# A third set of seven-product tiles, scaling on GpSimd and regrouped loads in a retention and feed-forward kernel

## The chip, the cores and the metric

The kernel runs on one NeuronCore of one Trainium2 chip. The metric is the device time of one execution, in microseconds (us), as the median of several executions; the profile is that of one more execution, read by the hardware profiler. PE is the matrix engine, ACT the scalar engine, DVE the vector engine, POOL is GpSimd, SP the sync engine, which only issues DMAs here.

## The reference

A retention layer (attention without softmax, with a decay per head) feeds a feed-forward layer:

```python
scores = scale * np.matmul(q, k.transpose(0, 1, 3, 2))      # q, k, v: 8 x 8 heads x 576 x 64
Dmat = np.where(rel >= 0, gamma[:, None, None] ** rel, 0.0) # rel = query position - key position
attn = np.matmul(scores * Dmat, v)
x = attn.transpose(0, 2, 1, 3).reshape(4608, 512)
h = x @ w_in                                                # 512 x 2048
out = (h * sigmoid(1.702 * h)) @ w_out                      # 2048 x 512
```

## The kernel before

**Tiling.** The 4608 tokens are 36 units of 128 tokens (`NU`), four units make one of nine chunks (`NCH`, c0 to c8). Units 8, 17, 26 and 35 hold the last 64 tokens of two batch entries each; their loads are split in two DMAs and they leave no state behind. For a unit u the kernel loads k, q (cast to bf16) and v by DMAs from POOL's queue (`load`, L925; `load_kq` L228, `load_v` L244), transposes k and q together by one DMA from SP's queue (`dma_transpose`, L399, key `T{u % 8}`), and scales v by a decay factor into `vp` (`scale_v`, L353, one 128x512 operation on DVE). Retention is done for two units at a time (`block`, L898): products with the state kept so far (`inter`), products with the masked scores of these units (`values`), and, in the same stretch of PE, the scores and the state contributions of the two units after them (`ahead`, L882). So the attention stretch of units 2j and 2j+1 reads the transposes and scaled v of units 2j+2 and 2j+3. On DVE it leaves two operations `x_out_pair` (L550, into xT), four `state_sum` (L442, running sums in the ring `stm` of 8 slots) and two `scores_out` (L514, masked scores); the sums are cast on ACT into `kv` (`state_cast`, L454).

**Up stage.** The hidden values of a chunk are 16 F tiles (f0 to f15) of 128 features by 512 tokens. A plain tile (`up`, L562) takes four products of 128x512 and one gelu on ACT out of PSUM into gT. In chunks 2 to 8 f0 to f7 are done in two `UpSet`s (L776) of four tiles each, by a scheme with seven block products in place of eight, where each block product (`step` n, n = 0 to 6) is four matmuls of 128x256. The operands are sums and differences of blocks of x (`xsums`, L764, four DVE operations per chunk) and of w_in (`winsums`, L745, four DVE operations once). A set uses two PSUM banks: X and Y for the first, C and D for the second. ACT copies steps 0, 2 and 3 out to `part`; DVE adds steps 1, 4 and 5 to these parts (`comb`, L811); ACT then makes the gelus: `gelu_first`, that of step 6 straight from PSUM, and `gelu_last` over two parts at once (128x1024).

**Down stage.** The product with w_out takes seven block products as well (`Pair.run`, L703), d1 to d7 below, of 16 matmuls of 128x256 each, that alternate between the banks A and B (`turn`, L862). d1 and d2 read gT as it is; d3 to d7 read sums that DVE made of gT (`Pair.sums`, L656: four operations 0 to 3, done for groups of F tiles). d3 needs operation 1, d4 operation 0, d5 operation 2 (which overwrites part of gT), d6 operation 3. The results are copied by ACT or added by DVE into `osb`, of which SP stores the rows. Between the products a function `hook(i)` (L1171) places other work; one attention stretch stands after d3 (hook 2). In the last chunk the tokens are two `Pair`s of single units.

**Order.** The order of each engine's queue is the order in which these calls are written; `Program.op` (L41) adds only the semaphore waits. So a wait at the head of a queue holds everything behind it. In a chunk of `steady` (L1070) from c2 on, SP is given four transposes (units 4c+6 to 4c+9), POOL is given the loads of units 4c+10 to 4c+13 to start once the last of these transposes has landed, and the four `scale_v` stand among the `comb`s and behind them (L1132 to L1142). The up stage runs the steps of its sets in turn, then the plain tiles in the banks A and B, with an attention stretch after the second of them (f13 in c2, f9 later; L1143 to L1153). All four sum operations of each group are given to DVE at the end of the up stage.

Of the kernel before, what the change touches and what calls it, by code (L numbers as in the profile page):

```python
# [13 lines left out]
P = 128  # L14
# [146 lines left out]
def bass_retnet_parallel__then__act_gelu_quick_kernel(  # L161
# [8 lines left out]
    NLD, NVN, NVP, NQT, NKV = 12, 10, 8, 8, 16  # L170
    es = ExitStack()
    with es:
        def sb(name, shape, dtype):
            return es.enter_context(nc.sbuf_tensor(name, shape, dtype))
# [13 lines left out]
        stm = sb("stm", [P, 8, HP, DH], FP32)  # L188
# [5 lines left out]
        winsum = sb("winsum", [P, 4, 2, 4, P], BF16)  # L194
# [247 lines left out]
        def state_sum(u, a):  # L442
            if u >= NU or unit_info(u)[1] == 2:
                return
            i = 2 * u + a
            src = ps32(KB[a])[:, 256 * (u % 2) : 256 * (u % 2) + 256].rearrange("p (a i) -> p a i", i=DH)
            dst, prev = stm[:, i % 8, :, :], stm[:, (i - 1) % 8, :, :]
            if unit_info(u)[2] == 0 and a == 0:
                op("dve", lambda e: e.tensor_copy(dst, src), reads=[KB[a]], writes=[f"stm{i % 8}"])
            else:  # L450
                op("dve", lambda e: e.tensor_tensor(dst, src, prev, ALU.add),  # L451
                   reads=[KB[a], f"stm{(i - 1) % 8}"], writes=[f"stm{i % 8}"])
# [6 lines left out]
        def cast_range(i0, n):  # L459
            op("act", lambda e: e.activation(  # L460
                kv[:, i0 % NKV : i0 % NKV + n, :, :], stm[:, i0 % 8 : i0 % 8 + n, :, :], AF.Copy),
               reads=[f"stm{(i0 + i) % 8}" for i in range(n)],
               writes=[f"kv{(i0 + i) % NKV}" for i in range(n)])
# [175 lines left out]
        class Pair:  # L639
# [16 lines left out]
            def sums(self, f0, f1):  # L656
                k0, k1 = f0 // 2, f1 // 2
                a, g = (lambda r, c: self.gpart(r, c, f0, f1)), (lambda r, c: self.gkeys(r, c, f0, f1))
                s = lambda n: gsum[:, n, k0:k1, self.at : self.at + self.n]
                ks = lambda n: [f"gs{n}_{k}_{j}" for j in self.places() for k in range(k0, k1)]  # L660
                for d, kd, x, kx, y, ky, alu in (
                    (s(0), ks(0), a(1, 0), g(1, 0), a(1, 1), g(1, 1), ALU.add),
                    (s(1), ks(1), s(0), ks(0), a(0, 0), g(0, 0), ALU.subtract),
                    (a(1, 0), g(1, 0), a(0, 0), g(0, 0), a(1, 0), g(1, 0), ALU.subtract),
                    (s(2), ks(2), a(0, 1), g(0, 1), s(1), ks(1), ALU.subtract),
                ):
                    op("dve", lambda e, d=d, x=x, y=y, alu=alu: e.tensor_tensor(d, x, y, alu),  # L667
                       reads=kx + ky, writes=kd)
# [76 lines left out]
        def winsums():  # L745
            def w(r, h):
                return w_in_sb[:, slice(h, 4, 2), 0 : 8 * P].rearrange(
                    "p a (k r n) -> p a k r n", r=2, n=P)[:, :, :, r, :]

            def ws(n):  # L750
                return winsum[:, n, :, :, :]

            for n, x, y, alu in ((0, w(1, 0), w(1, 1), ALU.add), (1, ws(0), w(0, 0), ALU.subtract),
                                 (2, w(0, 0), w(1, 0), ALU.subtract), (3, w(0, 1), ws(1), ALU.subtract)):
                op("dve", lambda e, n=n, x=x, y=y, alu=alu: e.tensor_tensor(ws(n), x, y, alu),
                   reads=[f"win{f}" for f in range(8)] + {1: ["wi0"], 3: ["wi1"]}.get(n, []), writes=[f"wi{n}"])
# [19 lines left out]
        class UpSet:  # L776
# [26 lines left out]
            def part(self, n):  # L803
                return (part[:, n, 512 * self.s : 512 * self.s + 512],
                        [f"gs{n}_{k}_{j}" for k in range(4 * self.s, 4 * self.s + 4) for j in range(2)])
# [48 lines left out]
            def gelu_last(self):  # L854
                v = part[:, 1:3, 512 * self.s : 512 * self.s + 512].rearrange("p n (i t) -> p n i t", t=256)
                self.gelu(v, self.part(1)[1] + self.part(2)[1], None, 1)

        SETS = (("X", "Y"), ("C", "D"))
        last_store = {}
# [210 lines left out]
        def steady():  # L1070
            four = Pair(0, 2, 2)
            for c in range(1, NCH):
                if c == 1:
                    for u in range(10, 14):
                        load(u)
                    for u in range(8, 14):
                        dma_transpose(u, [f"vn{13 % NVN}"])
                    for u in (14, 15):
                        load(u, after=[f"T{9 % NQT}_0"])
                else:  # L1080
                    for u in range(16 if c == 2 else 4 * c + 6, min(4 * c + 10, NU)):
                        dma_transpose(u)
                    for u in range(4 * c + 10, 4 * c + 14):
                        load(u, after=[f"T{(4 * c + 9) % NQT}_0"])
                last = c == NCH - 1
                if c == 1:
# [21 lines left out]
                    for u in (14, 15):  # L1108
                        dma_transpose(u)
                    for u in (16, 17):  # L1110
                        load(u, after=[f"T{15 % NQT}_0"])
                else:
                    pairs = (Pair(3, 0, 1), Pair(1, 2, 1, 1)) if last else (four,)
                    vps = [u for u in range(4 * c + 6, 4 * c + 10) if u < NU]
                    sets = [UpSet(c, i, *banks) for i, banks in enumerate(SETS)]
                    f0 = 4 * len(sets)

                    def sums(f0, f1, which=pairs):
                        for pair in which:
                            pair.sums(f0, f1)  # L1120

                    if c == 2:
                        for lo in (0, 2):
                            for f in (f0, f0 + 2):
                                up_group(c, f, 2, lo, lo + 2, turn())
                    for n in range(7):
                        for w in sets:
                            w.step(n)
                        if c == 2 and n == 1:
                            now(rest)  # L1130
                            rest.clear()
                        if n in ((3, 4) if c == 2 else (1, 4)):  # L1132
                            for u in vps[:1]:
                                scale_v(u)
                            del vps[:1]
                        if c == 2 and n == 4:
                            state_cast(12, 14)
                        if n in (4, 5):
                            for w in sets[:-1] if n == 4 else sets[-1:]:
                                w.gelu_first()  # L1140
                    for u in vps:
                        scale_v(u)  # L1142
                    for f in range(12 if c == 2 else 8, NF):  # L1143
                        up(c, f, b=turn())
                        if f == (12 if c == 2 else 9):
                            sets[0].gelu_last()
                            if not last:
                                rest = block(2 * c + 2)
                                now(rest[:2])
                                del rest[:2]  # L1150
                                sets[1].gelu_last()
                                now(rest[:4])
                                del rest[:4]  # L1153
                        if last and f == 11:
                            sets[1].gelu_last()
                        if f == (13 if c == 2 or last else 11):
                            sums(0, 8)
                            if last or c == 2:
                                sums(8, 12)
                    if last:  # L1160
                        sums(12, 16, pairs[:1])
                    else:
                        sums(12 if c == 2 else 8, 16)
# [7 lines left out]
                def hook(i):  # L1171
                    if c == 1:
# [15 lines left out]
                        if i == 5:  # L1188
                            scale_v(12)
                            scale_v(13)  # L1190
# [5 lines left out]
                    if i == 0:  # L1196
                        cast_now()
                        now(rest)
                        rest.clear()
                    if i == 2 and 2 * (2 * c + 3) < NU:  # L1200
                        rest.extend(block(2 * c + 3))
                        now(rest[:2])
                        del rest[:2]
# [3 lines left out]
                    if i == 4:  # L1207
                        now(xsums(c + 1))
                        cast_now()
                    if i == 5:  # L1210
                        now(rest)
                        rest.clear()

# [64 lines left out]
```

## Time and profile before

| quantity | value |
|---|---|
| runs | 285.85, 286.57, 289.94 us; median 286.57 |
| the profiled execution, its own time | 289.0 us |
| its span, first to last instruction | 287.2 us |
| PE busy | 273.8 us, 95% of the span |
| DVE busy | 201.5 us, 70% |
| ACT busy | 150.2 us, 52% |
| POOL busy (issuing DMAs, nearly all) | 110.2 us, 38% |
| mean granted clock of PE | 0.994 |

Busy shares are means over stages that differ. In the timeline a row gives the start, the duration, the engine, the line, the operation and its tiles, and in brackets the idle time before it and who ended it. Matmuls are pipelined: a group of matmuls lasts, for what comes behind it, from its start to the start of the next group, which is less than the duration in its row. The same holds for ACT and DVE, where the next operation starts before the row's end.

### The profile page before, as it was taken

The page shows a single profiled execution, that of the slowest core. Times are in us where ns is not written, and L with a number is a line of the kernel's source. Part 1 is how long each engine was busy: PE and PEld are TensorE (multiplying, and loading weights), DVE is VectorE, ACT ScalarE, POOL GpSimd, SP SyncE. Part 2 cuts the span into 40 slices and gives each one's busy share as a digit, 9 for nine tenths or more (in the row PEclk, how much of TensorE's full clock was granted, in tenths as well). Part 3 has the DMA queues.
Part 4 walks back from the last instruction along what each step waited for, and adds up shares of the span by engine and source line. Part 5 has one row for each costly group of instructions (what it writes and reads, how often), then busy time and mean ns, then how long its engine had stood idle before and what let it go on. Part 6 is the DMA issues. An engine that isn't in the chain of part 4 may idle for free.

```text
span 287.2 us, 9444 instructions
## 1 busy us (share of the span) xinstructions
PE 273.8 (95%) x4202; PEld 202.7 (71%) x4202; DVE 201.5 (70%) x402; ACT 150.2 (52%) x266; POOL 110.2 (38%) x141
## 2 busy tenths in 40 slices
PE   8899999999879969999999999999999999999996
PEld 6575445788768548866885788479848884887475
DVE  5851657598658795789778977877787876745541
ACT  7456333663318822585368536842774288327821
POOL 9999878103308193008604920093053000000000
PEclk9999999999999997999999999999999999999999
DMA  9999999999999899499967996599788090012013
GB/s 167 183 201 206 201 234 243 242 139 149 141 229 192 99 159 135 147 151 97 198 213 107 152 121 169 129 141 157 236 95 113 2 205 19 2 41 108 0 25 124
DMA packets 116937, 40.73 MB, mean 142 GB/s; under 512 B 104096, under 2 KB 110240, under 8 KB 116896
## 3 DMA queue, kind: packets, MB, share of 16 engines
q0 software_dynamic: 79712, 22.82, 70.7%
q1 hardware_dynamic: 36896, 17.05, 26.3%
q8 instruction: 33, 0.54, 0.8%
q10 hardware_dynamic: 288, 0.26, 0.3%
q14 instruction: 8, 0.07, 0.1%
HBM read 36.70 MB, written 9.44 MB: 161 GB/s over the span
## 4 chain that ended last, share of the span: by engine, by line
PE 56%; POOL 20%; DMA 13%; DVE 5%; ACT 3%; issue 2%; SPq 0%; POOLq 0%; DVEq 0%
PE psA L685 14%; PE psB L685 14%; POOL kqn L236 10%; DMA vn<-in_v_dram 7%; PE psB L566 6%; PE psA L566 6%; POOL vn L249 5%; PE psC L799 4%; PE psX L799 4%; DMA kqn<-in_q_dram 3%; PE psD L799 3%; DVE part L667 3%; PE psY L799 3%; DMA kqT<-kqn 3%; POOL w_in_sb L271 3%; ACT gT L822 2%
## 5 line engine op out<-in xcount | busy, mean ns | idle before, releaser
L236 POOL DMA_DIRECT2D kqn<-in_k_dram x39 | 34.3, 884 | 107.0 <-DMA kqT<-kqn 104.0
L249 POOL DMA_DIRECT2D vn<-in_v_dram x40 | 36.5, 921 | 0.2
L236 POOL DMA_DIRECT2D kqn<-in_q_dram x37 | 32.7, 893 | 0.1
L566 PE MATMUL psB<-xT,w_in_sb 128*128 128x512 bf16 x120 | 30.9, 380 | 0.4 <-ACT gT L571 0.4
L566 PE MATMUL psA<-xT,w_in_sb 128*128 128x512 bf16 x120 | 30.9, 380 | 0.3
L698 ACT ACTIVATE osb<-psA 128x512 f32<-128x512 f32 (+1 forms) x19 | 10.5, 552 | 37.4 <-PE psA L685 37.3
L355 DVE TENSOR_TENSOR vp<-vn,vfac 128x512 bf16<-128x512 f32 x36 | 23.9, 684 | 6.1 <-DMA vn<-in_v_dram 6.1
L698 ACT ACTIVATE osb<-psB 128x512 f32<-128x512 f32 (+1 forms) x17 | 9.3, 547 | 36.0 <-PE psB L685 36.0
L554 DVE TENSOR_TENSOR xT<-psX,gq 128x512 bf16<-128x512 f32 x16 | 11.1, 691 | 22.9 <-PE psX L529 22.9
L822 ACT ACTIVATE gT<-part 128x512 bf16<-128x512 f32 (+1 forms) x28 | 22.2, 847 | 0.0
L460 ACT ACTIVATE kv<-stm 128x1024 bf16<-128x1024 f32 (+1 forms) x17 | 15.4, 903 | 11.9 <-DVE stm L451 11.9
L571 ACT ACTIVATE gT<-psA 128x512 bf16<-128x512 f32 x30 | 17.9, 596 | 6.8 <-PE psA L566 6.6
L571 ACT ACTIVATE gT<-psB 128x512 bf16<-128x512 f32 x30 | 17.9, 596 | 6.5 <-PE psB L566 6.5
L566 PEld LDWEIGHTS psB<-xT,w_in_sb 128*128 128x128 bf16 x120 | 10.4, 98 | 15.2 <-ACT gT L571 5.5
L566 PEld LDWEIGHTS psA<-xT,w_in_sb 128*128 128x128 bf16 x120 | 10.4, 98 | 14.5 <-ACT gT L571 5.0
L685 PE MATMUL psB<-wsum,part 128*128 128x256 bf16 x128 | 16.6, 280 | 3.0 <-DVE part L667 3.0
L685 PE MATMUL psA<-wsum,gT 128*128 128x256 bf16 x144 | 17.5, 273 | 1.0 <-issue 1.0
L685 PEld LDWEIGHTS psB<-wsum,part 128*128 128x128 bf16 x128 | 12.1, 99 | 5.7 <-DVE part L667 4.1
L685 PE MATMUL psA<-wsum,part 128*128 128x256 bf16 x128 | 15.7, 275 | 0.3 <-DVE osb L701 0.3
L685 PEld LDWEIGHTS psA<-wsum,gT 128*128 128x128 bf16 x144 | 14.0, 98 | 2.9 <-issue 1.2
L667 DVE TENSOR_TENSOR part<-gT 128x1024 bf16<-128x1024 bf16 (+2 forms) x21 | 11.7, 559 | 5.7 <-ACT gT L571 4.6
L685 PE MATMUL psB<-w_out_sb,gT 128*128 128x256 bf16 x128 | 15.4, 273 | 0.0
(151 smaller groups left out, 679.4 us busy)
## 6 DMA issues: line engine op xcount, KB each, us to landing
vn<-in_v_dram POOLq DMA_DIRECT2D x32, 256.0 KB, 5.0
out_dram<-osb SPq DMA_DIRECT2D x30, 256.0 KB, 2.5
kqn<-in_k_dram POOLq DMA_DIRECT2D x31, 128.0 KB, 4.6
kqn<-in_q_dram POOLq DMA_DIRECT2D x31, 128.0 KB, 4.9
w_out_sb<-in_moe_w_out_dram POOLq DMA_DIRECT2D x4, 512.0 KB, 14.1
out_dram<-osb SPq DMA_DIRECT2D x10, 128.0 KB, 2.4
w_in_sb<-in_moe_w_in_dram POOLq DMA_DIRECT2D x8, 128.0 KB, 5.3
w_in_sb<-in_moe_w_in_dram POOLq DMA_DIRECT2D x4, 256.0 KB, 7.9
```

The lines of the kernel that those rows point to most:

```text
L236: e.dma_start(kqn[sl][p0 : p0 + n, which, :, :], src[b, :, s0 : s0 + n, :].rearrange("h p d -> p h d"),)
L249: e.dma_start(vn[sl][p0 : p0 + n, :, :], v[b, :, s0 : s0 + n, :].rearrange("h p d -> p h d"))
L355: op(eng, lambda e: e.tensor_tensor(vp[u % NVP].ap(), vn[sl].ap(), vfac[:, ty, :, None].to_broadcast([P, H, DH]), ALU.mult), reads=[f"vn{s ...
L460: op("act", lambda e: e.activation(kv[:, i0 % NKV : i0 % NKV + n, :, :], stm[:, i0 % 8 : i0 % 8 + n, :, :], AF.Copy), reads=[f"stm{(i0 + i ...
L554: op("dve", lambda e: e.tensor_tensor(xT[ch % 2][:, slice(hh, 4, 2), P * jj : P * jj + 2 * P].rearrange("p g (u t) -> p u g t", u=2), ps32 ...
L566: op("pe", lambda e, a=a: e.matmul(bank[b][:, n0:n1], w_in_sb[:, a, P * f : P * f + P], xT[c % 2][:, a, n0:n1], start=(a == 0), stop=(a == ...
L571: op("act", lambda e: e.activation(gT[:, f, n0:n1], bank[b][:, n0:n1], AF.Gelu_apprx_sigmoid), reads=[b], writes=[f"g_{f}_{j}" for j in ra ...
L667: op("dve", lambda e, d=d, x=x, y=y, alu=alu: e.tensor_tensor(d, x, y, alu), reads=kx + ky, writes=kd)
L685: op("pe", lambda e, x=x, y=y, t=t, s=not more and t == 0 and k == 0, z=k == NF // 2 - 1: e.matmul(bank[b][:, 256 * t : 256 * t + 256], x, ...
L698: op("act", lambda e: e.activation(dst[0], src[0], AF.Copy), reads=src[1], writes=dst[1])
L799: op("pe", lambda e, x=x, y=y, i=i, s=not more and i == 0 and k == 0, z=k == 1: e.matmul(bank[b][:, 256 * i : 256 * i + 256], x, y, start= ...
L822: op("act", lambda e: e.activation(dst, src, AF.Gelu_apprx_sigmoid), reads=reads, writes=[f"g_{f0 + 2 * i + q}_{j}" for i in range(2) for ...
```

## The change

F tiles 8 to 11 of chunks 3 to 8 become a third `UpSet`. It uses the two banks A and B, and rows 0, 2 and 3 of `osb` for its three parts; `winsums` makes its operands as well (128x1536 in place of 128x1024). The up stage of these chunks follows a written order: `sn` is step n of set s, `PB f` a plain tile in bank B, `F` and `L` the first and last gelu of a set, `@` the attention stretch with its two `x_out_pair`, `s2` two `state_sum`, `S` sums of the last chunk. In chunks 2 to 7 the sums of gT are split: operations 0 and 1 stay at the end of the up stage, 2 and 3 go behind the two `scores_out` after d2. `xsums` moves from hook 4 to hook 5, and the `scores_out` before it from hook 5 to hook 4. From unit 12 on v is scaled on POOL. Transposes and loads go in groups of four that begin at a multiple of four: transposes of 4c+8 to 4c+11 and loads of 4c+12 to 4c+15 in chunk c; in c1 the loads of units 12 to 15 wait for transpose 11, and the loads of 16 to 19 for transpose 15, with the four scalings of units 12 to 15 between them on POOL. The ring `stm` has 4 slots in place of 8.

```diff
-        winsum = sb("winsum", [P, 4, 2, 4, P], BF16)
+        winsum = sb("winsum", [P, 4, 2, 6, P], BF16)
...
             def part(self, n):
+                if self.s == 2:
+                    row = (0, 2, 3)[n]
+                    return osb[:, row, :], okeys(row)
...
+        ORDER = """00 10 01 11 PK12 02 12 PE13 03 13 F0 04 14 F1 20 05 15 21 06 16 L0 @0 22 23
+            L1 PX14 s2 24 F2 s2 25 S0 PY15 26 L2 S2"""
...
+            def transpose_and_load(c):
+                for u in range(4 * c + 8, min(4 * c + 12, NU)):
+                    dma_transpose(u)
+                for u in range(4 * c + 8, min(4 * c + 12, NU)):
+                    scale_v(u, "pool")
+                for u in range(4 * c + 12, 4 * c + 16):
+                    load(u, after=[f"T{(4 * c + 11) % NQT}_0"])
...
-                    for u in range(10, 14):
+                    for u in (10, 11):
                         load(u)
-                    for u in range(8, 14):
-                        dma_transpose(u, [f"vn{13 % NVN}"])
-                    for u in (14, 15):
-                        load(u, after=[f"T{9 % NQT}_0"])
+                    for u in range(8, 12):
+                        dma_transpose(u, [f"vn{11 % NVN}"])
+                    for u in range(12, 16):
+                        load(u, after=[f"T{11 % NQT}_0"])
...
-                    vps = [u for u in range(4 * c + 6, 4 * c + 10) if u < NU]
-                    sets = [UpSet(c, i, *banks) for i, banks in enumerate(SETS)]
+                    free = "AB" if turns[0] % 2 else "BA"
+                    sets = [UpSet(c, i, *banks) for i, banks in enumerate(SETS if c == 2 else SETS + (free,))]
...
+                        acts = {"F": lambda i: sets[i].gelu_first(), "L": lambda i: sets[i].gelu_last(),
+                                "@": lambda i: attend(), "s": lambda i: None if last else states(i),
+                                "S": lambda i: sums(4 * i, 4 * i + (4 if i == 2 else 8)) if last else None}
+                        for w in ORDER.split():
+                            if w[0] == "P":
+                                up(c, int(w[2:]), b=w[1])
+                            elif w[0] in acts:
+                                acts[w[0]](int(w[1:]))
+                            else:
+                                sets[int(w[0])].step(int(w[1]))
+                        if last:
+                            sums(12, 16, pairs[:1])
+                        else:
+                            sums(0, 8, which=(0, 1))
+                            sums(8, 16, which=(0, 1))
...
                     if i == 0:
                         cast_now()
+                    if i == 1:
                         now(rest)
                         rest.clear()
+                        for f0, f1 in ((0, 8), (8, 12), (12, 16)) if c == 2 else ((0, 8), (8, 16)):
+                            four.sums(f0, f1, (2, 3))
...
                     if i == 4:
-                        now(xsums(c + 1))
                         cast_now()
-                    if i == 5:
                         now(rest)
                         rest.clear()
+                    if i == 5:
+                        now(xsums(c + 1))
```

## The prediction

> **What bounds the kernel now.** I read the engine shares, then a table by stage, then the timeline of the stage that loses most, then one regular chunk, then the DMAs' landing times.
>
> ```profile
> PE 273.8 (95%) x4202; PEld 202.7 (71%) x4202; DVE 201.5 (70%) x402; ACT 150.2 (52%) x266; POOL 110.2 (38%) x141
> ```
>
> PE is the bound, but a mean hides the stages. The table's windows are cut at the first product of a down stage (c1, c2) or of an up stage (c3 on); columns are length, then busy us per engine, PE clock, DMA.
>
> ```profile
> 65.66:99.59 33.93, 30.65 (x634) 24.41 (x633) 23.93 (x45) 16.71 (x27) 12.25 (x16) 1.00 1.35 168
> 99.59:117.58 17.99, 15.31 (x225) 12.51 (x224) 14.85 (x33) 3.95 (x6) 10.38 (x12) 0.91 1.09 118
> 145.63:173.63 28.00, 27.98 (x450) 21.37 (x448) 22.76 (x43) 16.11 (x26) 12.05 (x15) 1.00 0.98 152
> 257.41:287.20 29.79, 26.11 (x202) 18.82 (x199) 12.77 (x36) 15.17 (x29) 0.00 (x0) 1.00 0.21 72
> ```
>
> From c3 on a chunk takes 28.00 with PE never free. The down stage of c2 (second row) takes 17.99; that of c4, 160.17 to 173.63, takes 13.46. These 4.53 are lost to DVE, with a clock of 0.91 in the window:
>
> ```profile
> 98.49 0.69 DVE L355 TENSOR_TENSOR vp<-vn,vfac 128x512 bf16<-128x512 f32 x1 [1.97 <-DMA vn<-in_v_dram]
> 102.00 0.68 DVE L667 TENSOR_TENSOR part<-gT 128x1024 bf16<-128x1024 bf16 x1
> 107.13 0.42 DVE L667 TENSOR_TENSOR part<-gT,part 128x512 bf16<-128x512 bf16 x1
> ```
> ```profile
> 106.93 1.89 PE L685 MATMUL psB<-wsum,part 128*128 128x256 bf16 x10 [1.07 <-DVE part L667]
> ```
>
> A late load of v stops DVE until 98.49; the twelve sum operations end at 107.55, and d3 on PE, due at 103.08, waits for them piece by piece. In the up stage of c2 PE loses 0.55 more to additions that stand behind scalings (93.19 to 93.58, 94.02 to 94.18). In c1 PE stands without a semaphore to wait for:
>
> ```profile
> 77.23 0.38 PE L685 MATMUL psA<-wsum,gT 128*128 128x256 bf16 x2 [1.02 <-issue]
> 83.97 0.22 PE L436 MATMUL psE<-vp,kqn 64*64 64x64 bf16 x2 [1.96 <-issue]
> ```
>
> Transposes land late while loads share the DMAs. Transposes' landing times from 60 to 100 us, where loads run beside them, and of four that run alone at 147:
>
> ```profile
> DMA to landing us min/median/max: 2.8/4.8/9.8
> ```
> ```profile
> DMA to landing us min/median/max: 2.8/2.8/2.9
> ```
>
> The prices of a regular chunk:
>
> ```profile
> 151.51 0.60 ACT L822 ACTIVATE gT<-psX 128x512 bf16<-128x512 f32 x1 [0.40 <-PE psX L799]
> 152.01 0.59 ACT L822 ACTIVATE gT<-psC 128x512 bf16<-128x512 f32 x1
> 154.17 1.99 ACT L822 ACTIVATE gT<-part 128x1024 bf16<-128x1024 f32 x2
> 154.92 0.69 DVE L554 TENSOR_TENSOR xT<-psX,gq 128x512 bf16<-128x512 f32 x1 [0.87 <-PE psX L529]
> 155.53 0.68 DVE L554 TENSOR_TENSOR xT<-psY,gq 128x512 bf16<-128x512 f32 x1
> 156.13 0.42 DVE L449 COPY stm<-psK 128x256 f32<-128x256 f32 x1
> 156.58 0.42 DVE L451 TENSOR_TENSOR stm<-psE,stm 128x256 f32<-128x256 f32 x1
> ```
>
> ACT begins 0.20 after PE ends (PE's last X product ends at 151.31), repeats every 0.50 (0.48 for copies), 0.57 for a first gelu, 0.95 for a double one, and lasts 0.60 or 1.05. DVE begins 0.21 after PE, repeats every 0.60 (0.45 for state sums), lasts 0.68. PE resumes 0.06 after either. On PE a step takes 0.44 (L799 groups at 145.63, 146.07), a plain tile 0.86 (L566 at 151.75, 152.61), the attention stretch 1.12 and 0.10 on either side.
>
> **The third set, c3 to c7.** Removed on PE: 16 matmuls of 0.216 = 3.46; added: 28 of 0.109 = 3.06. So 0.40 a chunk, 2.4 over six. ACT gains three copies, a first gelu, one from PSUM and a double one, and loses four gelus: +1.5 in a stage where it had 10.9 of work in 14.54. The written order, from t = 0 at step 00 (gaps only where named):
>
> - Steps and K, E up to 16: PE ends at 8.73. Gelu 06 starts on ACT at 8.50 (X ends 8.29), ends 9.10. The attention stretch needs bank X: it starts at 9.16, not 8.83. Wait 0.33.
> - 22, 23, X14, 24, 25, Y15, 26 follow; PE is done at 14.35.
> - DVE: the two x_out at 10.53 and 11.13, two state sums, the addition of 24 at 12.81, two state sums, the addition of 25 at about 14.21, done 14.90. d1 writes the bank that 25 used (the turn gives it that bank): it waits until 14.96, 0.6.
> - ACT: the last double gelu runs 15.07 to 16.11; DVE's operations 0 and 1 end at 17.55; d3 starts at 18.45. Hidden, 0.9 to spare.
>
> The up stage takes 14.96 against 14.54 (145.63 to 160.17): +0.42 in c3 to c6, +1.7 in all. Ends: -0.22 a chunk if the additions come in time (14.32), +0.9 if one 0.48 slot on ACT slips too. In c7 the second two state sums don't exist (unit 35), the addition of 25 ends at 14.1, d1 starts at 14.35: -0.2.
>
> **The split sums, xsums, the ring.** Operations 2 and 3 (four of 0.60) now stand between the scores_out and the x_out after d3. DVE is then busy without a gap from 18.65: 0.6 + 1.2 + 2.4 + 1.2 + 1.7, and its addition of d5 ends at 26.5 against d7's start at 26.77: hidden with 0.2 to spare, the thinnest cover here. xsums end 1.2 after the next chunk's start, step 02 needs them at 2.61. The stores move 0.3 later on SP, the transposes behind them too; these have 8 us until d3. Four ring slots: the cast that frees them is over 6 us earlier. Larger winsums: 4 x 0.3 at 60.6, sums 0.6 later, d3 of c1 at 69.75 has 1.2 to spare. All nothing.
>
> **Scaling on POOL.** No such row exists. Below: DVE's 0.60. Above: POOL's 128x128 iota takes 0.237, so two inputs of 512 one after the other 1.9. I take one stream, 0.95, the nearest POOL row. They stand on POOL behind 12 load issues of 0.87, and nobody needs them for 10 us. But in c4 the transposes land early (9 after the start), the scalings fall at 20 to 24, on the thin cover above. If DVE's sums wait one for one, d7 is 4 x 0.6 - 0.2 = 2.2 late; if not, 0. I take 0.7.
>
> The Trainium skill, GPSIMD Engine Reference, section 3.1, has 4497 ns for 2048 fp32 elements, an estimate of 1.12 here; it would leave the sum as it is. The Trainium skill, SBUF — State Buffer, section "SBUF: two separate sides", speaks against the change: a GpSimd operation and a DVE operation with two SBUF inputs take turns for whole instructions. By it c4 would lose the full 2.2, and the sums of c2 as much; the trace of before has no pair to show it.
>
> **c2.** Gone: the four scalings and the late v from DVE. The x_out then start at 96.4, the sums' first halves end at 102.4, d3 comes at 102.53: the 0.55 and the 4.53 go, -5.1. Late next: d3's attention stretch needs transpose 17 at about 105.8. The loads of 16 to 19 wait for transpose 15 (below), start at about 90, q of 17 is issued at 94 and lands 4.3 to 9.2 later, its transpose 2.8 to 9.8 after that: 101 to 113. Wait 0 to 7; with the median 4.8 it lands at 105: I take 1.5, collisions on POOL in it. Net -3.6.
>
> **c1.** The v load of unit 11, issued at 44.67, lands after 13.7, at 58.4 (v of 13: 63.08). Four transposes take 6.9 alone (147.39 to 154.28), up to 1.5 more with pauses like that of 64.62 (an issue of 2.12 in place of 1.27): 67. Twelve loads follow; q of 13 is issued at 70.7 and lands at 75.0 to 79.9, transpose 13 at 77.8 to 89.7. Block 5 needs it at 82 (before: 81.03, and the pause at 76). It replaces a wait that lasted until 83.97: -2.0 to +5.7. Middle of both ranges 77.5 + 4.8 + 1.2 for a pause = 83.5, no change; as the range leans late, +1.0.
>
> **c8.** No attention here, so ACT is the chain: from gelu 06 at 8.50 it has two gelus, a double, two copies, a double, X14, a first gelu, Y15 and 26 without a gap (7 x 0.48 + 0.57 + 2 x 0.95 = 5.83), and the last double ends 1.05 later, at 15.38. d1 begins with unit 3's tokens, whose f8 that gelu gives: at 15.44. DVE's 20 sum operations (8 of 0.37 from 12.9 on, then 12 of 0.23, spacings as at 269 to 274) then end at 18.64, the addition of d2 at 19.06, d4 starts at 19.12. Before: 274.77 - 257.41 = 17.36. +1.8; ends +1.0 and +2.6, one double either way.
>
> **Sum.** c1 +1.0, c2 -3.6, c3 to c6 +1.7, c4 +0.7, c7 -0.2, c8 +1.8: +1.4 on the profiled execution's 289.0 (span 287.2 and 1.8 around it). That execution is 2.4 over the median of 286.57; set on the median, 288.0.
>
> **Rivals.** (1) Nothing new waits: -5.1 - 2.4 = -7.5, and c1 unchanged: 279.1. For it: PE really has less to do. Against: the additions stand behind state sums in DVE's queue. It needs the addition of 25 by 14.29 and the last gelu of c8 1.8 earlier. (2) Late transposes: twice as many loads run beside the transposes of c1 and c2. If transpose 13 lands after 85, every us later is one lost, and 17 follows: +4.5 and +3.5 beyond my values, 296.0. Over 2% begins where both together exceed 4.3 more. For it: the 9.8 above. Against: the 2.8. (3) POOL and DVE collide in every chunk: 2.2 in c2 to c5 less the 0.7 counted, 296.1; against: only c4's scalings fall on the thin cover. (4) The set saves nothing but the rest comes: my forecast.
>
> **How the numbers follow.** Forecast 0.52 (284.5 to 291.5 by its bounds); rival 1, 0.13; rival 2, 0.22; rival 3, 0.13. 2% of 286.57 is 5.7, about what a measurement of this kernel can tell. Faster: most of rival 1, 0.10. Slower: 0.16 of rival 2, 0.07 of 3, 0.23. Same 0.67. Range 283.5 to 294.0: half-way to rival 1, three quarters of the way to rivals 2 and 3, about 2 in 10 left outside.
>
> **What would show it.** Right: in c3 to c6 a wait of d1 for DVE's addition and of the attention stretch for the gelu of X; d1 of c8 waiting for the double gelu; d3 of c2 without a wait. Wrong: chunks under 27.8; scores waiting for kqT before 110; DVE's sums longer beside POOL's scalings.

## The result, and where the time went

The changed kernel takes 304.84 us (median of 4 runs, 302.25 to 306.44) against 287.0 for the kernel before (4 runs, 285.85 to 289.94): a ratio of 1.060, 95% interval 1.048 to 1.071. The forecast of 288.0 is wrong, and so is its range (283.5 to 294.0). The profiled execution took 306.13 (span 303.7), before 289.0 (span 287.2): 17.1 more, where the sum had 1.4.

First line of the page of the changed kernel:

```profile
PE 274.9 (91%) x4253; PEld 212.7 (70%) x4274; DVE 212.6 (70%) x396; ACT 156.3 (51%) x278; POOL 137.9 (45%) x165
```

PE's busy time rose by 1.1, its share fell from 95% to 91%: PE stands and waits. The table by stage says where. Both kernels are cut here at the first product of each down stage (columns: length, busy us of PE, PEld, DVE, ACT, POOL, PE clock, DMA, GB/s); the kernel after:

```profile
65.60:101.73 36.13, 31.60 (x633) 25.28 (x634) 24.76 (x47) 16.50 (x27) 27.86 (x32) 0.95 1.41 169
101.73:131.66 29.93, 28.04 (x452) 22.67 (x452) 23.85 (x42) 16.11 (x28) 17.38 (x19) 1.00 1.47 166
131.66:165.49 33.83, 30.33 (x458) 23.89 (x461) 25.11 (x42) 16.75 (x28) 21.89 (x26) 0.90 1.20 153
165.49:196.41 30.92, 27.89 (x444) 22.46 (x444) 23.56 (x38) 17.72 (x30) 16.15 (x18) 1.00 0.92 139
196.41:231.14 34.73, 30.05 (x458) 23.23 (x460) 26.92 (x41) 16.70 (x29) 12.29 (x14) 0.95 0.72 113
231.14:258.89 27.75, 27.38 (x442) 22.77 (x445) 21.52 (x39) 16.53 (x28) 0.00 (x0) 1.00 0.12 40
```

Beside the lengths of the same stretches before, and what the prediction's terms make of each:

| stretch | before | after | difference | predicted |
|---|---|---|---|---|
| c1 down, c2 up | 33.93 | 36.13 | +2.2 | +0.45 (+1.0 - 0.55) |
| c2 down, c3 up | 32.58 | 29.93 | -2.65 | -2.6 (-3.05 + 0.42) |
| c3 down, c4 up | 28.00 | 33.83 | +5.8 | +0.4 |
| c4 down, c5 up | 28.00 | 30.92 | +2.9 | +1.1 (0.7 + 0.42) |
| c5 down, c6 up | 28.00 | 34.73 | +6.7 | +0.4 |
| c6 down, c7 up | 28.00 | 27.75 | -0.25 | -0.2 |
| c7 down, c8 | 43.03 | 44.81 | +1.8 | +1.8 |

Where POOL issues nothing any more (the last two rows) the forecast holds to 0.1. Nearly all of the error lies in four of the five stretches where POOL and the DMAs work.

**c4 and c5: DVE's sums beside POOL's scalings.** DVE's timeline in the down stage of c5 (start, duration), then POOL's:

```profile
201.92 1.82 DVE L668 TENSOR_TENSOR gT<-gT 128x1024 bf16<-128x1024 bf16 x1
203.67 0.68 DVE L668 TENSOR_TENSOR part<-gT,part 128x1024 bf16<-128x1024 bf16 x1
204.27 2.53 DVE L668 TENSOR_TENSOR gT<-gT 128x1024 bf16<-128x1024 bf16 x1
206.72 2.53 DVE L668 TENSOR_TENSOR part<-gT,part 128x1024 bf16<-128x1024 bf16 x1
209.17 0.68 DVE L554 TENSOR_TENSOR xT<-psX,gq 128x512 bf16<-128x512 f32 x1
```
```profile
202.35 1.50 POOL L249 DMA_DIRECT2D vn<-in_v_dram  x2
203.74 4.96 POOL L355 TENSOR_TENSOR vp<-vn,vfac 128x512 bf16<-128x512 f32 x4
```

In the kernel before no sum took over 0.694. Here two take 2.53 beside the four scalings, and one 1.82 that begins while POOL still issues loads. The x_out behind them, which reads PSUM, takes its 0.68. What stands behind in DVE's queue comes 4.8 later, and PE's last product of the stage, d7, waits for it:

```profile
212.80 0.57 PE L686 MATMUL psA<-wsum,gT 128*128 128x256 bf16 x2 [2.02 <-DVE osb L702]
```

In c5 PE loses 0.91, 0.77, 0.69 and 2.18 (between the groups of d4, d5, d6 and d7), and d7 then takes 3.24 for the usual 1.75, at a granted clock of 0.51: 6.0 of the 6.3 above forecast. In c4, with sums of 0.95 to 1.53, it loses 0.66 and 1.88. In c2 and c3 four sums are held as well (1.26 to 2.42), but PE waits only 0.3 for them.

**c4's up stage: PE stops inside a product.** PE's weight loads of step 23:

```profile
155.95 0.21 PEld L800 LDWEIGHTS psB<-xsum,winsum 128*128 128x128 bf16 x2
159.30 0.31 PEld L800 LDWEIGHTS psB<-xsum,winsum 128*128 128x128 bf16 x2 [3.15 <-issue]
```

Between the second and third weight load of one product there is no semaphore: PE waits for nothing that the profile's list of releasers shows, which is what "<-issue" means. What the DMAs carried while it stood (157.05 to 159.25; queue, packets, MB, share), and how the transposes of that chunk fared:

```profile
q1 hardware_dynamic: 1031, 0.26, 127.7%
q8 instruction: 1, 0.02, 2.7%
```
```profile
L401 SPq DMA_TRANSPOSE kqT<-kqn x4: 2138/2924/3167, 147.3 to 156.6; - x4
DMA to landing us min/median/max: 4.1/7.5/9.7
```

A packet of 16 KB of instructions passes here, 16 us after the one before it. It lands at 158.02, and PE goes on 1.3 later. Around it transposes take 7.5 in place of 2.8: loads of units 24 to 27, the stores and the transposes of the chunk all run between 147 and 157. The stop (3.15) and the steps behind it, which run at half clock (0.50 in the window 160 to 164), are the 5.4 above forecast:

```profile
160.00:164.00 4.00, 3.78 (x14) 1.95 (x14) 1.27 (x3) 2.65 (x4) 2.94 (x4) 0.50 0.57 47
```

**c1** shows the wait that the prediction worked out, scores of block 5 for transpose 13, with its end at the middle of the range. What c1 and c2's up stage lose beyond it comes later: a stop of 1.24 without a semaphore at 101.08 and a mean clock of 0.92 from 83.59 on. **c6 and c8** show the small waits that it worked out (gelu on X, addition of step 25, the last double gelu):

```profile
83.59 0.26 PE L507 MATMUL psC<-kqT 64*64 64x64 bf16 x1 [2.74 <-DMA kqT<-kqn]
...
101.08 0.81 PE L566 MATMUL psA<-xT,w_in_sb 128*128 128x512 bf16 x3 [1.24 <-issue]
...
225.35 0.21 PE L491 MATMUL psX<-kqT,kv 64*64 64x64 bf16 x1 [0.25 <-ACT gT L827]
...
231.14 0.61 PE L686 MATMUL psB<-w_out_sb,gT 128*128 128x256 bf16 x4 [0.44 <-DVE osb L818]
...
287.56 0.61 PE L686 MATMUL psB<-w_out_sb,gT 128*128 128x256 bf16 x4 [1.52 <-ACT gT L827]
```

### The profile page after: what moved, and what is told of

It reads as the page before. It is cut to its first block, busy times and chain, and to the rows that moved or that the text cites. A ratio compares the mean times of both kernels' runs of the same rounds, so it can differ in the third digit from the quotient of the medians.

```text
span 303.7 us, 9652 instructions
## 1 busy us (share of the span) xinstructions
PE 274.9 (91%) x4253; PEld 212.7 (70%) x4274; DVE 212.6 (70%) x396; ACT 156.3 (51%) x278; POOL 137.9 (45%) x165
## 4 chain that ended last, share of the span: by engine, by line
PE 52%; DVE 15%; POOL 15%; DMA 10%; issue 4%; ACT 2%; SPq 1%; POOLq 0%
PE psA L686 12%; PE psB L686 10%; POOL kqn L236 7%; DVE part L668 5%; DMA vn<-in_v_dram 5%; DMA kqT<-kqn 4%; PE psX L800 4%; POOL vn L249 4%; PE psC L800 3%; PE psD L800 3%; PE psY L800 3%; PE psB L800 3%; PE psA L800 3%; DVE gT L668 2%; POOL w_in_sb L271 2%
## 5 line engine op out<-in xcount | busy, mean ns | idle before, releaser
L355 POOL TENSOR_TENSOR vp<-vn,vfac 128x512 bf16<-128x512 f32 x24 | 28.1, 1196 | 22.2 <-DMA vn<-in_v_dram 18.3
L686 PE MATMUL psA<-wsum,gT 128*128 128x256 bf16 x144 | 19.2, 289 | 2.8 <-DVE osb L702 2.0
L818 DVE TENSOR_TENSOR part<-psX,part 128x512 f32<-128x512 f32 x7 | 4.8, 689 | 16.9 <-PE psX L800 16.9
L686 PE MATMUL psA<-w_out_sb,gT 128*128 128x256 bf16 x128 | 15.5, 273 | 0.9 <-DVE osb L818 0.9
L668 DVE TENSOR_TENSOR part<-gT,part 128x1024 bf16<-128x1024 bf16 (+2 forms) x21 | 16.0, 764 | 0.0
L580 PE MATMUL psB<-xT,w_in_sb 128*128 128x256 bf16 x112 | 15.4, 283 | 0.5 <-DMA w_in_sb<-in_moe_w_in_dram 0.5
L668 DVE TENSOR_TENSOR gT<-gT 128x1024 bf16<-128x1024 bf16 (+2 forms) x21 | 15.8, 751 | 0.0
L686 PE MATMUL psB<-wsum,gT 128*128 128x256 bf16 x112 | 13.7, 273 | 2.2 <-DVE osb L702 1.7
L686 PEld LDWEIGHTS psB<-w_out_sb,gT 128*128 128x128 bf16 x128 | 12.3, 98 | 4.1 <-ACT gT L827 1.8
L580 PE MATMUL psA<-xT,w_in_sb 128*128 128x256 bf16 (+1 forms) x120 | 13.9, 260 | 1.2 <-DMA w_in_sb<-in_moe_w_in_dram 0.9
```

The source lines that it names most:

```text
L355: op(eng, lambda e: e.tensor_tensor(vp[u % NVP].ap(), vn[sl].ap(), vfac[:, ty, :, None].to_broadcast([P, H, DH]), ALU.mult), reads=[f"vn{s ...
L580: op("pe", lambda e, a=a, f=f, i=i: e.matmul(bank[b][:, n * i : n * i + n], w_in_sb[:, a, P * f : P * f + P], xT[c % 2][:, a, P * lo : P * ...
L686: op("pe", lambda e, x=x, y=y, t=t, s=not more and t == 0 and k == 0, z=k == NF // 2 - 1: e.matmul(bank[b][:, 256 * t : 256 * t + 256], x, ...
```

## The experiments

Three causes stand against each other: P (POOL's scalings hold DVE's sums), D (regrouped loads and transposes run late and together), S (the third set and its order cost more than worked out). Each run has the kernel before beside it on its chip (287.7, 287.7 and 287.3 in the three groups of runs).

**e1, scaling of units 20 to 35 back on DVE.**

```diff
-                for u in range(4 * c + 8, min(4 * c + 12, NU)):
+                for u in range(4 * c + 8, min(4 * c + 12, NU if c < 3 else 0)):
                     scale_v(u, "pool")
...
-        ORDER = """00 10 01 11 PK12 02 12 ... 20 05 15 21 06
+        ORDER = """00 10 01 11 V2 PK12 02 12 ... 20 05 15 V2 21 06
...
```

> The changed kernel, but V of units 20 to 35 (the chunks 3 to 6) is scaled on DVE in the up stage, two after step 11 and two after step 15, instead of on POOL. Theory P (POOL's scalings hold DVE's sums): the four sums that took 1.5 to 2.5 us in chunks 4 and 5 go back to 0.68, and the waits of PE for them there go (0.66 + 1.88 in chunk 4, 0.91 + 0.77 + 0.69 + 2.18 in chunk 5, and the 1.5 that the eighth product of chunk 5 lost to half clock): 8.6 less, about 296. Theory D (the regrouped loads and transposes are late, and that alone costs): these waits go elsewhere or stay, 303 to 306. The 3.1 us stop of PE in the up stage of chunk 4 stays by both, or grows where DVE now waits for a late v.

Measured: 299.86, ratio 1.042 (1.038 to 1.046); between the two. No sum of c3 to c8 is long, and c4 to c6 take 28.5, 28.4 and 28.9. But the late loads hit DVE now, in c3, and PE behind it:

```profile
126.18 0.69 DVE L355 TENSOR_TENSOR vp<-vn,vfac 128x512 bf16<-128x512 f32 x1 [0.65 <-DMA vn<-in_v_dram]
131.40 0.69 DVE L355 TENSOR_TENSOR vp<-vn,vfac 128x512 bf16<-128x512 f32 x1 [4.53 <-DMA vn<-in_v_dram]
132.00 0.68 DVE L818 TENSOR_TENSOR osb<-psA,osb 128x512 f32<-128x512 f32 x1
```
```profile
132.75 0.61 PE L800 MATMUL psA<-xsum,winsum 128*128 128x256 bf16 x2 [4.80 <-DVE osb L818]
```

P is right for c4 and c5; D costs by itself, here 4.80 in c3 and 3.9 in c1 (transpose 13). The stop in c4, which was expected to stay, did not come; that the stall in c3 had let the loads finish first is likely, but no run tests it.

**e2, POOL's scaling moved to the up stage.**

```diff
...
-                    scale_v(u, "pool")
+                    scale_v(u, "pool", [f"T{u % NQT}_0"] if c > 2 else [])
```

> The changed kernel, but POOL's scaling of units 20 to 35 waits for the unit's transpose, so that it runs in the up stage of the chunk, beside DVE's additions out of PSUM, and no longer beside the sums of the down stage. Theory P with the hold confined to DVE operations that read SBUF alone: no sum over 0.7 us, 8.6 less, about 296, as with the scaling on DVE. If POOL's scaling holds every DVE operation: the additions of the up stage take 1.5 to 2.5 us, each step behind them slips, and the time stays at 303 to 308. Theory D: 303 to 306.

Measured: 301.44, ratio 1.045 (1.040 to 1.050). The span's account: P's 8.6 of c4 and c5 is gone (c5 and c6 begin 28.4 and 29.0 after the chunk before), but transpose 13 came later still, and PE waited 7.0 for it in place of 2.9 (gaps between products; the list of waits has 6.8 and 2.7): -8.6 + 4.1 = -4.5, where the span lost 5.4. The stop at step 23 of c4 is there, 3.65. The expectation missed by taking c1's wait as fixed.

**e3, the old groups, all else as changed.**

```diff
...
-                for u in range(4 * c + 8, min(4 * c + 12, NU)):
+                us = range(16 if c == 2 else 4 * c + 6, min(4 * c + 10, NU))
+                for u in us:
                     dma_transpose(u)
...
-                for u in range(4 * c + 12, 4 * c + 16):
-                    load(u, after=[f"T{(4 * c + 11) % NQT}_0"])
+                for u in range(4 * c + 10, 4 * c + 14):
+                    load(u, after=[f"T{(4 * c + 9) % NQT}_0"])
...
```

> The changed kernel with the loads and transposes in the groups of before (units 4c+6 to 4c+9 transposed, 4c+10 to 4c+13 loaded), scaling still on POOL in front of the loads of the next group. Theory D: no wait for transpose 13, no stop of 3.1 us in the up stage of chunk 4 and no half clock after it; 2.9 + 1.4 + 1.1 in chunks 1 and 2 and 5.4 in chunk 4 less, so 294 to 297, with the long sums still there. Theory P: the sums still collide with the scalings, which still follow the loads; if P were all, 303 to 306.

Measured: 295.94, ratio 1.028 (1.020 to 1.036). D is right: no wait for transpose 13, no stop in c4. What stays is P, in c3, c4 and c5 (d7 waits 1.31, 1.89, 1.10). DVE and PE in c4:

```profile
164.63 2.54 DVE L668 TENSOR_TENSOR gT<-gT 128x1024 bf16<-128x1024 bf16 x1
167.09 1.52 DVE L668 TENSOR_TENSOR part<-gT,part 128x1024 bf16<-128x1024 bf16 x1
```
```profile
172.17 0.39 PE L686 MATMUL psB<-wsum,gT 128*128 128x256 bf16 x2 [1.72 <-DVE osb L702]
```

**e8, the old groups and POOL's scaling in the up stage** (e3 with e2's edit).

> The run with the old groups (295.9, sums beside scalings held to 1.5 to 2.5 us), but POOL's scaling of units 18 on waits for the unit's transpose and so runs in the up stage. Theory P: the waits of 1.31, 1.89 and 1.10 of the eighth product in chunks 3 to 5 go, and with them all that the old groups left: 288 to 291, as with scaling on DVE (289.5). If scaling on POOL costs beyond those sums: 293 or more.

Measured: 288.94, ratio 1.004 (1.000 to 1.009). That is 7.0 less than e3. By the two traces 5.4 of it lies in c3 to c5 (29.96, 30.82 and 30.08 in e3; 28.51, 28.35 and 28.61 here), and that is P. The other 1.6 lies mostly before c3, where the two kernels are the same. Beside POOL's scalings DVE now has operations that read PSUM, and these are not held. DVE and POOL in the up stage of c3, and one of DVE's four groups of sums over the whole run (duration min/median/max in ns; the longest of any is 694):

```profile
122.04 0.69 DVE L554 TENSOR_TENSOR xT<-psX,gq 128x512 bf16<-128x512 f32 x1 [1.58 <-PE psX L529]
122.65 0.68 DVE L554 TENSOR_TENSOR xT<-psY,gq 128x512 bf16<-128x512 f32 x1
```
```profile
120.43 3.04 POOL L355 TENSOR_TENSOR vp<-vn,vfac 128x512 bf16<-128x512 f32 x3 [0.62 <-DMA kqT<-kqn]
```
```profile
L668 DVE TENSOR_TENSOR gT<-gT x21: 284/681/685, 65.0 to 272.4; 128x1024 bf16<-128x1024 bf16 x13, 128x512 bf16<-128x512 bf16 x4, 128x256 bf16<-128x256 bf16 x4
```

The scalings take 1.01 each here, and 1.24 each beside the sums of c5 above: both sides wait.

**e4, the set and the halved sums alone** (old groups as in e3, scaling on DVE as in e1).

> The third set with its written order, the four-slot ring and the sums in two halves alone: loads and transposes in the groups of before, all scaling on DVE (in the up stage, at about the places of before). Theory S (the set costs what the prediction said): 0.42 in each of chunks 3 to 6, -0.2 in 7, 1.8 in 8, against it some 2 to 3 gained in the down stage of chunk 2: 285 to 289 against 287 before. If the set or its order has another cost, over 291. If both P and D are right, the whole of the loss is gone here.

Measured: 289.5, ratio 1.006 (1.003 to 1.010); just above the range's end. From c3's down stage to c4's, and the last down stage:

```profile
128.49:156.97 28.48, 27.79 (x460) 22.79 (x461) 24.51 (x45) 17.14 (x29) 12.61 (x17) 1.00 1.02 161
...
268.82:287.10 18.28, 12.91 (x114) 10.62 (x111) 8.61 (x30) 5.14 (x12) 0.00 (x0) 1.00 0.19 58
```

28.48 is the 28.00 + 0.42 of the prediction, 18.28 the 16.01 + 2.27 of c8 (with c7 0.5 shorter: +1.8). S costs what was worked out, and e5 below agrees: it has the halved sums without the set and the four-slot ring, and e4 takes 3.0 more, where the prediction's terms for the set make 3.3 (1.7 - 0.2 + 1.8). Of the change's 17.1 that is the part of the products themselves.

**e5, before with the sums in halves alone.**

```diff
...
+                    if i == 1:
                         now(rest)
                         rest.clear()
+                        for f0, f1 in ((0, 8), (8, 12), (12, 16)) if c == 2 else ((0, 8), (8, 16)):
+                            four.sums(f0, f1, (2, 3))
...
```

> The kernel before, with one part of the change alone: the sums in two halves (operations 2 and 3 after the second product's hook, the x sums one hook later). Two sets, DVE scaling and the old groups stay. In the run with set and sums, the down stage of chunk 3 began 3.7 earlier than before, and the rest cost 3.6 more. If the halves give the first and the set the second: 283 to 284.5. If the early part came from the set or the smaller ring: 286 to 288.

Measured: 286.46, ratio 0.996 (0.992 to 1.000), in the second range and 2 above the first. Yet the trace is that of the first: the halves do end c2's wait of d3 (c2 down with c3 up takes 28.01 in place of 32.58), and later chunks take 28.1, near the 28.00 of before. Part of this gain is lost again in the stretch before, c1 down with c2 up, which takes 35.71 in place of 33.93, at a clock of 0.95 in place of 1.00:

```profile
65.12:100.83 35.71, 32.04 (x632) 25.29 (x633) 25.78 (x49) 16.71 (x27) 16.32 (x20) 0.95 1.21 168
```

And the profiled execution of before is 1.3 over the median of the runs beside this one; part of its wait in c2 may be that execution's own late load, and then counts less in the median; no run here settles how much.

**e6, e2 with the first loads as before.**

```diff
-                    for u in (10, 11):
+                    for u in range(10, 14):
                         load(u)
                     for u in range(8, 12):
-                        dma_transpose(u, [f"vn{11 % NVN}"])
-                    for u in range(12, 16):
+                        dma_transpose(u, [f"vn{13 % NVN}"])
+                    for u in range(14, 16):
                         load(u, after=[f"T{11 % NQT}_0"])
```

> The run with POOL's scaling in the up stage (301.4, where PE waited 7.0 for transpose 13 and 3.7 with no work at hand in chunk 4), but the first loads are those of before: units 10 to 13 ahead of transposes 8 to 11, 14 and 15 behind them. From chunk 2 on the groups stay the changed ones. Theory D1 (all lateness stems from the start: transposes 12 to 15 wait for loads that wait for transpose 11): both waits go and the time is 288 to 292. Theory D2 (groups from a multiple of four are late by themselves, since two units more must be fetched by the end of chunk 2): the wait for transpose 13 goes, one in chunk 2 or 3 or the stop in chunk 4 stays, 293 to 297.

Measured: 293.22, ratio 1.016 (1.009 to 1.024): D2. c1 has no wait over 0.4 left (c1 down with c2 up takes 31.12). In c4 the stop is back, at the same place in the code as in the changed kernel and 3.4 earlier in the time; its c4 stretch takes 35.42:

```profile
155.95 0.32 PEld L800 LDWEIGHTS psB<-xsum,winsum 128*128 128x128 bf16 x2 [4.36 <-issue]
```

Loads of units 24 to 27, two more than before had asked for by then, still run when this chunk's stores and transposes start (141.8 on), and the transposes take 7.7 in the middle.

**e9, e6 with 44 of the matmuls left out that only warm PE up at 3.3 us.**

```diff
-            warm(44, "A", 64)
```

> The run with the first loads early (293.2; in chunk 4 PE stands still for 4.35 from 151.60, between two weight loads of one product, step 23, without a semaphore to wait for), with 44 of the matmuls left out that only warm PE up at 3.3 us. Theory I (PE's instructions are fetched by DMA, in packets of 16 KB that stand behind the mixed loads and transposes): the place where the packet is needed moves 44 matmuls on, to about the second product of the down stage, which PE reaches after the transposes have landed at 157; no stop at step 23 (another may show where a packet now falls, in the attention stretch of chunk 4 or in chunk 1), 286 to 290. Theory II (the stop belongs to step 23, its operands or its bank): 4 us at the same step, 292 to 295.

Measured: 294.67 (2 runs), ratio 1.026 (1.018 to 1.033). The time lies in the range of theory II, and what theory I gave is missed; but the mechanism of theory I is what the trace shows. Step 23 of c4 runs through. The stop is in c3's attention stretch, 6.2 long, amid transposes that take up to 14.2:

```profile
128.37 0.21 PE L529 MATMUL psX<-pm,vp 64*64 64x64 bf16 x1 [6.21 <-issue]
```
```profile
L401 SPq DMA_TRANSPOSE kqT<-kqn x4: 1232/4156/6067, 114.2 to 130.0; - x4
DMA to landing us min/median/max: 4.3/11.5/14.2
```

From 107.5 to 125.9 the DMAs carried no packet on queue q8, which brings instructions in 16 KB packets; from 122.1 to 128.3 one:

```profile
q0 software_dynamic: 2136, 0.54, 115.9%
q1 hardware_dynamic: 1035, 0.26, 57.6%
q8 instruction: 1, 0.02, 1.0%
```

Leaving out work that has nothing to do with c3 or c4 moved the stop from one to the other: it belongs to PE's place in its instruction stream, not to an operand. The times of the packets say the same. In the thirteen traces PE has 17 pauses of 1 us or more after the first 20 us that are put down to issue, and each ends 1.3 to 1.8 us after a 16 KB packet has landed (here 127.05 and 128.37; in the changed kernel 99.50 and 101.08, 158.02 and 159.30; in the kernel before 75.80 and 77.23, 82.58 and 83.97). That PE waits for the packet is shown by this; that mixed loads and transposes make the packet late is what the places of the stops point to. The Trainium skill, Advanced Engine Details and Errata, section "ISA Cache", has a line of 16 KB for 256 instructions. This case agrees roughly: 33 such packets in the changed kernel, whose page counts 4253 + 4274 rows on PE and its weight loads, 258 to a packet.

**e7, e4 with another order, and two sets in c8.**

```diff
-        ORDER = """00 10 01 11 V2 PK12 02 12 PE13 03 13 F0 04 14 F1 20 05 15 V2 21 06 16 L0 @0 22 23
-            L1 PX14 s2 24 F2 s2 25 S0 PY15 26 L2 S2"""
+        ORDER = """00 10 01 11 V2 PK12 02 12 PE13 03 13 F0 04 14 F1 05 15 V2 06 20 16 21 L0 @0 22 23
+            L1 PX14 s2 24 F2 25 s2 PY15 26 L2"""
...
-enumerate(SETS if c == 2 else SETS + (free,))
+enumerate(SETS if c == 2 or last else SETS + (free,))
...
```

> The run with set and sums (289.5), with another written order in chunks 3 to 7: step 06 in front of 20 and 16 in front of 21, so that the gelu on X ends before the attention stretch, and the last state sums behind the addition of step 25; chunk 8 takes two sets, as before. Theory S (the set loses 0.33 and 0.6 in a chunk to waits for ACT and DVE, 1.8 in chunk 8, and saves 0.4 on PE): four times 0.6, five times 0.33 and 1.8 less, 282.5 to 285. If the waits only change their place (scores that wait for the gelu on C, a state cast late): 286 to 289.

Measured: 284.95, ratio 0.990 (0.986 to 0.994), at the upper edge of the first range. Both regular waits (gelu on X, addition of step 25) are gone from the profile; a chunk without another stop takes 27.40 (156.82 to 184.22), 0.6 less than before. In c1 PE still stopped for 3.7 without a semaphore.

**e10 and e11, what the runs point to.** e11 is e7 with the first transposes and loads of e6 and the old groups from c2 on (scaling on DVE); e10 has POOL's scaling in the up stage as well.

```diff
-                    for u in range(8, 14):
+                    for u in range(8, 12):
                         dma_transpose(u, [f"vn{13 % NVN}"])
                     for u in (14, 15):
-                        load(u, after=[f"T{9 % NQT}_0"])
+                        load(u, after=[f"T{11 % NQT}_0"])
...
-                    for u in (14, 15):
+                    for u in range(12, 16):
                         dma_transpose(u)
```

> What the runs point to: sums in halves, the third set with the other order, two sets in chunk 8, the old groups from chunk 2 on but the first transposes 12 and 13 behind those of 8 to 11 and all of 8 to 11 ahead of the loads of 14 and 15, scaling on POOL in the up stage from unit 18 on. From the parts: chunk 3's down stage at 125.8 (first loads early), then the stages of the run with the other order (28.2, 27.4, 28.9, 27.5, 27.0) and 16.0: 281 for the span, 282 to 284.5 as a median. If the gain of the early loads needs the groups of four: 285 to 287.

> The run with the other order and two sets in chunk 8 (284.95; PE stood 3.85 in chunk 1 without a semaphore), scaling on DVE, with only the first transposes moved: 8 to 11 ahead of the loads of 14 and 15, 12 and 13 in the down stage. If the stop in chunk 1 comes from loads and transposes that run together: 281 to 283. If it moves to another place: 284 to 286.

Measured: e10 283.85, ratio 0.987 (0.981 to 0.992); e11 282.91, ratio 0.987 (0.982 to 0.992). Both beat the kernel before by 1.3%, and cannot be told apart. The page of e11 has PE at 96%:

```profile
PE 269.9 (96%) x4262; PEld 209.6 (75%) x4262; DVE 211.4 (76%) x417; ACT 155.4 (56%) x276; POOL 110.1 (39%) x141
```

In e11 the stop in c1 is gone (c1 down with c2 up takes 31.22, in e7 35.79), as it was expected if mixed loads and transposes make it; one of 1.0 is left in c6. In the medians e7 and e11 are not clearly apart (ratios 0.990 and 0.987). In e10 two stops, of 1.8 and 0.9, stand in c2's up stage and in c6.

## Why the prediction was wrong

- **"Scaling on POOL ... But in c4 ... the thin cover above": mis-sized, and its place misread.** It priced the hold at 0.6 for each of four sums and let it end at c4. Measured, a sum of c4 or c5 loses up to 1.85, since two scalings can pass before it; and c5 has loads too (units 32 to 35), behind which four scalings fall 7 to 12 us after the down stage's first product, as in c4 (6 to 12). The term was 0.7 and measured 8.6 (2.5 in c4, 6.0 in c5, 1.5 of that half clock after the waits). The rule of the Trainium skill that it weighed (SBUF — State Buffer, "SBUF: two separate sides": a GpSimd operation and a DVE operation with two SBUF inputs take turns) agrees with e3 and e8 in kind: sums out of SBUF 1.52 to 2.54 beside scalings, operations out of PSUM 0.68. Its own rival 3 had the mechanism, at 2.2 for each of four chunks; it came as 2.5 and 6.0 in two.
- **"The stores move 0.3 later on SP, the transposes behind them too; these have 8 us until d3 ... All nothing": the other step that failed.** Beyond c2 the regrouping of loads and transposes has no term in the prediction: it took them to mix in c1 and c2 only. The groups from a multiple of four ask for two units more by the end of c2, and that lag is carried on: in c3 and c4 loads still run when the transposes start. c4's up stage paid 5.4. And the two pauses "<-issue" that the prediction showed in c1 were counted as a pause of about 1, not read as what they are, PE waiting for its instructions (e9), which can fall on any chunk. That is the path that it had wrong: late transposes cost little by waits for their data and much by stops of PE beside them; with the old groups (e3) the one in c4 is gone.
- **c1, +1.0 in a range of -2.0 to +5.7: the wait right, the rest not foreseen.** The wait for transpose 13 ended at 83.59, where 83.5 was worked out. With c2's up stage the stretch was still 1.75 over, by the stop of 1.24 at 101.08 and the lower clock, for which there was no term. In e2 the same wait was 7.0: the wide range was needed.
- **c2, -3.6: right in size, in part by luck.** -2.65 for its down stage and c3's up stage, forecast -2.6. But the 1.5 in it was to be a wait for transpose 17, and none came; PE lost about as much to a stop of 0.93 without a semaphore (until 109.31) and to smaller waits. In the median of runs the halves are worth less: e5, which has them alone, gains 1.2.
- **The third set, c7 and c8: right.** 14.99 for the up stage of c6 where 14.96 was worked out; -0.25 for c7's stretch; +1.8 for c8; e4 shows them alone.
- **The chances.** Rivals 2 and 3 were held to be alternatives, each with +8. Rival 3's mechanism came. Rival 2 as written did not: transpose 13 was there by 83.59 and not after 85, and nothing waited for transpose 17; the regrouping cost by another path. That 288.0 + 8.0 + 8.1 = 304.1 lies near the 304.84 measured is therefore luck. What holds is that two costs at different places came together, and the range had no room for both.

What stays open: why a sum in c5 took 1.82 while POOL only issued loads (201.92 above), when other sums beside load issues took 0.69; how far ahead PE's packets are asked for, which sets where a stop falls; and which of the mixed DMAs makes a packet late.

## What to carry to other kernels

Work moved to an idle engine is not free where it holds up the engine that it leaves: place it beside operations that read PSUM, not beside those that read SBUF alone (e3 to e8: 5.4 us in c3 to c5). A regrouping of transfers that only asks for more, earlier, shifts every later transfer; follow it to the chunk where the lag is gone before costing it at nothing. And two rivals at different places in the time can both come: a range must reach to their sum.

## What the runs showed of the hardware

- A DVE operation of 0.68 on SBUF data alone took up to 2.62 beside POOL's tensor operations of about 1.0 to 1.5 (e1, in c2); one that reads PSUM kept its 0.68 (e8).
- PE stood up to 6.2 us in the middle of a stretch with no semaphore to wait for, while loads and transposes shared the DMAs (e9); 44 matmuls fewer at the start moved the stop by a chunk. Every such pause of 1 us or more ended 1.3 to 1.8 us after a 16 KB packet of instructions had landed.
- The transposes of one chunk took 2.8 to 3.2 us from issue to landing alone (e8, 140 to 148) and 4.3 to 14.2 beside loads and stores (e9); POOL's scaling of 128x512 took 1.04 where nothing held it (e8), near the estimate of 1.12 that the prediction worked out from the Trainium skill's GPSIMD Engine Reference, section 3.1, and not the 0.95 that it took.
